# First head mixing as three float32r passes, with a hi/lo split of the gathered scores

## Chip, cores, metric
One core of a Trainium2 chip. The metric is the device time of one launch in microseconds (us), the median of several runs; lower is better.

## What is computed
Two batches, 12 heads, 448 positions, head size 64. Scores are mixed over the heads, go through a softmax, are mixed over the heads again and multiply v; two feed-forward blocks follow. The part before them:

```python
scores = scale * np.matmul(q, k.transpose(0, 1, 3, 2))
scores = np.einsum('bhij,hg->bgij', scores, w_pre)
scores = scores - np.max(scores, axis=-1, keepdims=True)
attn = np.exp(scores)
attn = attn / (np.sum(attn, axis=-1, keepdims=True) + 1e-09)
attn = np.einsum('bhij,hg->bgij', attn, w_post)
return np.matmul(attn, v).astype(np.float32)
```

## The kernel before
Queries of a batch are cut into four tiles of 120, 120, 120 and 88 rows (`tiles`, index `ti`). `qk` (L134) makes the raw scores of two heads of a tile with float32 matmuls. `qk_out` (L145) copies them to SBUF, the even head on ScalarE (L153), the odd one on VectorE (L151), into one of four `s` buffers, and SyncE's DMA queue scatters them into a gather tile `G` (two of them, used by even and odd tiles) whose partitions hold 10 query rows times 12 heads. The 88-row tile needs three DMAs per head (L157, L165) where the others need one.

The mixing then runs over 46 pairs of such groups (`PAIRS`, `plist`): 6, 6, 6 and 5 pairs per batch; a tile's pair index r is 0 for its first pair, and the 88-row tile's last pair holds one group only. `premix` (L167) multiplies a group by the head weights in one float32 matmul, which the trace shows as two records. `smin` (L176, VectorE) and `sexp` (L183, ScalarE) are the softmax, `weights2` (L193, VectorE) folds 1/sum into the second mixing weights w2, `post` (L208) is the second mixing, and `evac` (L225) copies its result out, half on ScalarE and half on VectorE. `av` (L245) multiplies by v, `av_out` (L259) copies that out.

Slot n of the main loop (L429) does: premix of pair n+1, `qk_out`, post of pair n, softmax of pair n+1, evac of n, weights2 of n+1, and then what hand-written tables put there (`at`, L302): `qk` of the next tile, `av` of the tile before, loads. `load_v` (L128) for the second batch is in the table of slot 29; it follows that slot's scatters on the DMA queue, and the first user is `av` in slot 30. In slots 37 to 43 (`dve_l`, and L413) ScalarE, VectorE and GpSimd also split the first weights of the feed-forward part and the attention output of batch 0 into float32r hi and lo parts (L372, L377, L401, L402). Every engine works strictly in the order of this program.

The feed-forward part (`stage`, L468; `mm`, L445) already multiplies in three float32r passes, hi·hi, hi·lo and lo·hi.

Of the kernel before, what the change touches and what calls it, by code (L numbers as in the profile page):

```python
# [8 lines left out]
F32R = mybir.dt.float32r  # L9
# [3 lines left out]
ALU = mybir.AluOpType  # L13
AX = mybir.AxisListType

B, H, S, D = 2, 12, 448, 64
# [11 lines left out]
GP = 128  # L28
JP = 112
NJ = S // JP  # L30
NC = DM // 128
# [8 lines left out]
PAIRS = []  # L40
# [12 lines left out]
def place(k, h):  # L53
    return 64 if (k, h) == (ROW - 1, H - 1) else PK * k + h
# [3 lines left out]
def attention_moe_kernel(  # L58
# [10 lines left out]
    nc = tc.nc  # L69
    ctx.enter_context(tc.manual_schedule())  # L70

    const = ctx.enter_context(tc.tile_pool(name="const", bufs=1))
# [4 lines left out]
    def ps(tag):  # L77
        return psum.tile([128, 512], F32, tag=tag, name=tag, bufs=PB[tag])

    def rd(ap):  # L80
        return ap.bitcast(F32)


    wpre_sb = const.tile([128, 128], F32, name="wpre_sb")
    wp = const.tile([128, H, KG], F32, name="wp")

    def single(tag, dtype=F32R):
        return outer.tile([128, S], dtype, tag=tag, name=tag)
# [10 lines left out]
    att = ExitStack()  # L99
    sb = att.enter_context(tc.tile_pool(name="att", bufs=1))  # L100
    s_p = att.enter_context(tc.tile_pool(name="s", bufs=4))
    e_p = att.enter_context(tc.tile_pool(name="e", bufs=2))
    a_p = att.enter_context(tc.tile_pool(name="a", bufs=2))

    G = [sb.tile([128, H, S], F32, name=f"G{i}") for i in range(2)]
    A = {}
    E = {}
    Z = {}
    W2 = {}
# [22 lines left out]


    def qk(b, t, c, tags=("qk", "qk")):  # L134
        n = ROWS[t]
        p = [ps(tag) for tag in tags]
        for e in range(2):
            o = 64 * e
            nc.tensor.matmul(  # L139
                p[e][0:n, 0:S], qq[b, t][o:o + 64, c * TILE:c * TILE + n], kk[b, c][o:o + 64, :], start=True, stop=True  # L140
            )
        for e in range(2):
            Sps.append((b, t, 2 * c + e, p[e]))

    def qk_out(stage=None):  # L145
        while Sps:
            b, t, h, p = Sps.pop(0)
            n = ROWS[t]
            s = stage[h // 2][0:TILE, h % 2, :] if stage else s_p.tile([TILE, S], F32, tag="s", name="s")
            if h % 2:  # L150
                nc.vector.tensor_copy(s[0:n], p[0:n, 0:S])  # L151
            else:
                nc.scalar.copy(s[0:n], p[0:n, 0:S])  # L153
            g = G[t % 2]
            full = n // ROW
            last = ROW - 1 if h == H - 1 else ROW
            nc.sync.dma_start(out=g[h:PK * (last - 1) + h + 1:PK, 0:full, :], in_=s[0:last * full])  # L157
            if last < ROW:
                o = place(last, h)
                nc.sync.dma_start(out=g[o:o + 1, 0:full, :], in_=s[last * full:ROW * full])  # L160
            rem = (n - full * ROW) // 2
            for f in range(2 if rem else 0):
                o = full * ROW + f * rem
                a = place(f * KG, h)
                nc.sync.dma_start(out=g[a:a + PK * (rem - 1) + 1:PK, full, :], in_=s[o:o + rem])  # L165

    def premix(b, m):  # L167
        t, r, n = PAIRS[m]
        for i in range(n):
            p = ps("T")  # L170
            nc.tensor.matmul(  # L171
                p[0:GP, 0:S], wpre_sb[0:GP, 0:GP], G[t % 2][0:GP, r + i, :], start=True, stop=True
            )
            Tps[b, m, i] = p

    def smin(b, m, i):  # L176
        if i == 0:
            NB[b, m] = e_p.tile([128, 2], F32, tag="nb", name="nb")
        nc.vector.tensor_reduce(  # L179
            out=NB[b, m][0:GP, i:i + 1], in_=Tps[b, m, i][0:GP, 0:S], op=ALU.min, axis=AX.X  # L180
        )

    def sexp(b, m, i):  # L183
        if i == 0:
            Z[b, m] = e_p.tile([128, 2], F32, tag="z", name="z")
        e = e_p.tile([128, S], F32, tag=f"e{i}", name="e")
        nc.scalar.activation(  # L187
            out=e[0:GP], in_=Tps.pop((b, m, i))[0:GP, 0:S], func=ACTF.Exp, bias=NB[b, m][0:GP, i:i + 1], scale=-1.0,
            accum_out=Z[b, m][0:GP, i:i + 1],
        )  # L190
        E[b, m, i] = e

    def weights2(b, m):  # L193
        n = PAIRS[m][2]
        z = Z.pop((b, m))[0:GP, 0:n]
        NB.pop((b, m))
        w2 = e_p.tile([128, 2, H * KG], F32, tag="w2", name="w2")
        nc.vector.tensor_scalar(z, z, 1e-9, None, ALU.add)
        nc.vector.reciprocal(out=z, in_=z)
        nc.vector.tensor_tensor(  # L200
            out=w2[0:GP, 0:n, :],
            in0=wp[0:GP].rearrange("p (o g) k -> p o (g k)", o=1).to_broadcast([GP, n, H * KG]),
            in1=z.rearrange("p (n o) -> p n o", o=1).to_broadcast([GP, n, H * KG]), op=ALU.mult,
        )
        W2[b, m] = w2


    def post(b, m):  # L208
        t, r, n = PAIRS[m]
        w2 = W2.pop((b, m))  # L210
        p = [ps("post") for _ in range(2)]
        k = H * KG
        for i in range(n):
            e = E.pop((b, m, i))
            for j in range(NJ):
                for f in range(2):
                    o = 64 * f
                    c = (i * NJ + j) * k
                    nc.tensor.matmul(  # L219
                        p[f][0:JP, c:c + k], e[o:o + 64, j * JP:(j + 1) * JP], w2[o:o + 64, i, :],  # L220
                        start=True, stop=True,
                    )
        Pps[b, m] = p

    def evac(b, m, f):  # L225
        t, r, n = PAIRS[m]
        if r == 0 and f == 0:
            A[b, t] = a_p.tile([JP, NJ * H, TILE], F32, tag="a", name="a")
        a = A[b, t]
        p = Pps[b, m][f]  # L230
        k = half_rows(t, r + n - 1)
        src = p[0:JP, 0:n * NJ * H * KG].rearrange("p (n g k) -> p n g k", n=n, k=KG)[:, :, :, 0:k]
        o = r * ROW + f * k
        dst = a[:, :, o:o + (n - 1) * ROW + k]
        if n == 2:
            dst = a[:, :, r * ROW:(r + 2) * ROW].rearrange("p g (n i) -> p n g i", n=2)[:, :, :, f * KG:f * KG + KG]
        else:
            src = src[:, 0]
        if f:
            nc.vector.tensor_copy(dst, src)  # L240
        else:
            nc.scalar.copy(dst, src)


    def av(b, t, c):  # L245
# [5 lines left out]
        for j in range(NJ):  # L251
            for e in range(2):
                g = 2 * c + e
                nc.tensor.matmul(  # L254
                    p[64 * e:64 * e + 64, o:o + n], vv[b][:, j, g * D:(g + 1) * D], A[b, t][:, j * H + g, 0:n],
                    start=(j == 0), stop=(j == NJ - 1), skip_group_check=True,
# [17 lines left out]
    nc.gpsimd.memset(G[0], 0.0)  # L274
    nc.vector.memset(G[1], 0.0)
    nc.vector.tensor_scalar(wpre_sb, wpre_sb, -0.125, None, ALU.mult)


    def busy(n):
# [16 lines left out]
    plist = [(b, m) for b in range(B) for m in range(NPB)]  # L296
    span = [sum(1 for x in PAIRS if x[0] == t) for _, t in tiles]
    base = [sum(span[:i]) for i in range(len(tiles))]
    NS = len(plist)
    act_l, dve_l, mid = {}, {}, {}  # L300

    def at(d, slot, *f):  # L302
        d.setdefault(max(slot, 0), []).append(f)

    for ti, (b, t) in enumerate(tiles):
        s0, sp = base[ti], span[ti]
        if ti + 1 < len(tiles):
            nxt = tiles[ti + 1]
            for c in range(NC):
                at(mid, s0 - 3 + c if ti else (c * (sp - 3)) // NC, qk, *nxt, c)  # L310
            if ti + 2 < len(tiles):
                at(mid, s0 - 2, load_q, *tiles[ti + 2])
            if nxt[1] == NTL - 1 and nxt[0] + 1 < B:
                for c in range(NC):
                    at(mid, s0 + c // 2, load_k, nxt[0] + 1, c)
        if ti > 0:
            pb, pt = tiles[ti - 1]
            for c in range(NC):
                s = s0 + 1 + (c * (sp - 1)) // NC
                at(mid, s, av, pb, pt, c)  # L320
                if c % 2:
                    at(mid, s, av_out, pb, pt, c // 2)
            if pt == NTL - 1 and pb + 1 < B:
                at(mid, s0 + sp, load_v, pb + 1)
# [80 lines left out]
    s0 = base[-1]  # L405
# [10 lines left out]
    def run(d, n):  # L416
        for f in d.get(n, []):
            f[0](*f[1:])

    def softmax(n):  # L420
        b, m = plist[n]
        for i in range(PAIRS[m][2]):
            smin(b, m, i)
            sexp(b, m, i)

    premix(*plist[0])
    softmax(0)
    weights2(*plist[0])
    for n in range(NS):  # L429
        if n + 1 < NS:  # L430
            premix(*plist[n + 1])
        qk_out()
        post(*plist[n])
        if n + 1 < NS:
            softmax(n + 1)
        run(act_l, n)
        evac(*plist[n], 0)
        evac(*plist[n], 1)
        if n + 1 < NS:
            weights2(*plist[n + 1])  # L440
        run(dve_l, n)
        run(mid, n)
# [204 lines left out]
```

## Time and profile before

| | us |
|---|---|
| median of 3 runs (771.75 to 772.64) | 772.56 |
| the profiled execution | 769.89 |
| its span, first to last instruction | 768.1 |
| attention part, to the first feed-forward matmul | 262.82 |
| TensorE busy in the span | 745.7 (97%) |
| TensorE's share of the chain that ended last | 95% |
| VectorE / ScalarE / GpSimd busy | 487.4 / 309.1 / 18.0 |

The sum of the prediction is made against the profiled execution, which is shorter than the median of the runs; the span lies inside it with 1.79 us around it. "PE" is TensorE's matmuls, "PEld" its weight loads, "DVE" VectorE, "ACT" ScalarE, "POOL" GpSimd, "SPq" the DMA issues of SyncE.

### The profile page before, as it was taken

Reading aid. Unit: us, or ns where it says so; the run is one execution under the profiler, and the core shown is the slowest. Engines: PE = TensorE matmul, PEld = TensorE weight load, DVE = VectorE, ACT = ScalarE, POOL = GpSimd, SP = SyncE. Lnnn points to the kernel's source line nnn. Section 1 sums busy time; section 2 is a strip of 40 time slices with the busy share of each in tenths; the row PEclk is TensorE's granted clock in tenths of the full one; section 3 lists DMA queues with packets and bytes.
Section 4 is the critical chain, followed back from the end, with each engine's and each line's share of the span. In section 5 each row is a group of like instructions: output and inputs, shape, how many; then the busy total and the mean of one; then the engine's idle time right before and its main releaser. Section 6 shows DMA issues by size and latency. Waiting matters only on the chain.

```text
span 768.1 us, 12411 instructions
## 1 busy us (share of the span) xinstructions
PE 745.7 (97%) x5055; PEld 617.8 (80%) x5055; DVE 487.4 (63%) x817; ACT 309.1 (40%) x559; POOL 18.0 (2%) x16
## 2 busy tenths in 40 slices
PE   6799999998999999999999999999999999999998
PEld 2356666665667799999999999999999999999997
DVE  4366656565667767676667666556888888654540
ACT  2355554454456443334333323223555554322220
POOL 3000000000002300000000000000000000000000
PEclk9799999999999999999999999999999999999999
DMA  6543243426141113323323323323233332434310
GB/s 215 170 132 102 82 129 116 120 74 188 57 146 58 61 65 125 123 83 123 124 83 124 123 83 124 124 82 124 83 123 101 106 124 88 160 129 134 126 48 36
DMA packets 26696, 84.85 MB, mean 110 GB/s; under 512 B 2896, under 2 KB 16736, under 8 KB 26416
## 3 DMA queue, kind: packets, MB, share of 16 engines
q1 hardware_dynamic: 26496, 83.59, 33.2%
q8 instruction: 40, 0.66, 0.4%
q0 software_dynamic: 144, 0.47, 0.2%
q14 instruction: 16, 0.13, 0.0%
HBM read 62.03 MB, written 2.75 MB: 84 GB/s over the span
## 4 chain that ended last, share of the span: by engine, by line
PE 95%; DMA 2%; SPq 1%; DVE 1%; ACT 0%; issue 0%; ACTq 0%; POOLq 0%
PE T L171 10%; PE post L219 10%; PE T L448 8%; PE T L449 8%; PE T L450 8%; PE qk L448 5%; PE post L449 5%; PE post L448 5%; PE post L450 5%; PE qk L449 5%; PE qk L450 5%; PE av L254 5%; PE qk L139 5%; PE av L450 3%; PE av L449 3%; PE av L448 3%
## 5 line engine op out<-in xcount | busy, mean ns | idle before, releaser
L372 ACT CAST wh<-wc 128x768 fp32r<-128x768 f32 x68 | 56.8, 835 | 122.3 <-DVE wc L366 108.8
L219 PEld LDWEIGHTS post<-w,e 64*112 64x112 f32 x1440 | 74.4, 174 | 29.8 <-PE T L171 21.5
L377 DVE TENSOR_TENSOR wl<-wc,wh 128x768 fp32r<-128x768 f32 x66 | 63.0, 955 | 48.1 <-ACT wh L372 48.1
L187 ACT ACTIVATE e<-T,nb 128x448 f32<-128x448 f32 x90 | 56.9, 633 | 88.0 <-DVE nb L179 87.9
L171 PE MATMUL T<-G,wpre_sb 128*128 128x448 f32 x180 | 82.3, 581 | 8.4 <-DMA G<-x 8.4
L449 PE MATMUL T<-m,wh 128*128 128x448 f32 x237 | 86.6, 365 | 0.0
L448 PE MATMUL T<-m,wh 128*128 128x448 f32 x237 | 86.6, 365 | 0.0
L450 PE MATMUL T<-m,wl 128*128 128x448 f32 x237 | 86.5, 365 | 0.0
L219 PE MATMUL post<-w,e 64*112 64x60 f32 x1440 | 80.5, 261 | 0.1
L179 DVE TENSOR_REDUCE nb<-T 128x1 f32<-128x448 f32 x90 | 55.8, 623 | 28.3 <-PE T L171 23.4
L171 PEld LDWEIGHTS T<-G,wpre_sb 128*128 128x128 f32 x180 | 31.6, 195 | 47.4 <-issue 46.1
L355 DVE SCALAR_TENSOR_TENSOR wa<-wr,wa 128x768 uint32<-128x768 uint32 x68 | 65.2, 959 | 2.3
L366 DVE SCALAR_TENSOR_TENSOR wc<-wc,wa 128x768 uint32<-128x768 uint32 x68 | 65.2, 958 | 2.3
L240 DVE COPY a<-post 112x480 f32<-112x480 f32 (+1 forms) x46 | 30.9, 671 | 49.6 <-PE post L219 49.6
L350 ACT ACTIVATE wc<-wr 128x768 f32<-128x768 f32 x68 | 61.4, 903 | 0.0
L254 PE MATMUL av<-a,v 112*64 112x120 f32 (+1 forms) x768 | 45.2, 264 | 5.2 <-DMA v<-v 3.0
L254 PEld LDWEIGHTS av<-a,v 112*64 112x64 f32 x768 | 37.0, 136 | 15.7 <-PE post L219 4.0
L362 DVE TENSOR_SCALAR wc<-wc 128x768 f32<-128x768 f32 x68 | 38.7, 569 | 16.3 <-ACT wc L350 16.3
L139 PE MATMUL qk<-ks,q 64*120 64x448 f32 (+1 forms) x176 | 44.9, 568 | 4.1 <-DMA q<-qT 2.3
L448 PEld LDWEIGHTS T<-m,wh 128*128 128x128 f32 x237 | 44.5, 188 | 3.5
L449 PEld LDWEIGHTS T<-m,wh 128*128 128x128 f32 x237 | 44.5, 188 | 3.5
L450 PEld LDWEIGHTS T<-m,wl 128*128 128x128 f32 x237 | 44.5, 188 | 3.5
(146 smaller groups left out, 1353.2 us busy)
## 6 DMA issues: line engine op xcount, KB each, us to landing
wr<-w SPq DMA_DIRECT2D x68, 768.0 KB
G<-s SPq DMA_DIRECT2D x55, 210.0 KB
G<-s SPq DMA_DIRECT2D x22, 140.0 KB
ks<-kT SPq DMA_DIRECT2D x12, 224.0 KB
v<-v SPq DMA_DIRECT2D x2, 1344.0 KB
outT<-ta SPq DMA_DIRECT2D x12, 224.0 KB
q<-qT SPq DMA_DIRECT2D x7, 360.0 KB
G<-x SPq DMA_DIRECT2D x11, 210.0 KB
```

The source lines that it names most:

```text
L139: nc.tensor.matmul(p[e][0:n, 0:S], qq[b, t][o:o + 64, c * TILE:c * TILE + n], kk[b, c][o:o + 64, :], start=True, stop=True)
L171: nc.tensor.matmul(p[0:GP, 0:S], wpre_sb[0:GP, 0:GP], G[t % 2][0:GP, r + i, :], start=True, stop=True)
L187: nc.scalar.activation(out=e[0:GP], in_=Tps.pop((b, m, i))[0:GP, 0:S], func=ACTF.Exp, bias=NB[b, m][0:GP, i:i + 1], scale=-1.0, accum_out= ...
L219: nc.tensor.matmul(p[f][0:JP, c:c + k], e[o:o + 64, j * JP:(j + 1) * JP], w2[o:o + 64, i, :], start=True, stop=True,)
L254: nc.tensor.matmul(p[64 * e:64 * e + 64, o:o + n], vv[b][:, j, g * D:(g + 1) * D], A[b, t][:, j * H + g, 0:n], start=(j == 0), stop=(j == ...
L350: nc.scalar.activation(out=st["c"], in_=rd(st["high"]), func=ACTF.Abs, scale=HSC)
L355: nc.vector.scalar_tensor_tensor(out=a, in0=st["high"], scalar=0x80000000, in1=a, op0=ALU.bitwise_and, op1=ALU.bitwise_or)
L366: nc.vector.scalar_tensor_tensor(out=cu, in0=cu, scalar=3, in1=st["a"], op0=ALU.logical_shift_left, op1=ALU.bitwise_or)
L377: eng.tensor_tensor(out=lo, in0=st["c"], in1=rd(st["hi"]), op=ALU.subtract)
L448: nc.tensor.matmul(p[:, 0:S], hi[:, sl], x[0], start=first, stop=False)
L449: nc.tensor.matmul(p[:, 0:S], hi[:, sl], x[1], start=False, stop=False)
L450: nc.tensor.matmul(p[:, 0:S], lo[:, sl], x[0], start=False, stop=last)
```

## The change
The head weights are split once into `wpre_hi` and `wpre_lo`. Each gathered group is split by `split_g`: ScalarE casts it to float32r (hi), GpSimd subtracts (lo). `premix` becomes hi·hi, lo·hi and hi·lo in one PSUM accumulation. The split of pair n+2 is issued in slot n, ahead of `qk_out`'s copies, or behind them where the pair is its tile's first. `qk` of the next tile moves one slot earlier, and calls `qk_out` first, so that a slot with several `qk` copies the earlier ones at once. There is one hi buffer per group index and two lo buffers.

```diff
+    wpre_hi = const.tile([128, 128], F32R, name="wpre_hi")
+    wpre_lo = const.tile([128, 128], F32R, name="wpre_lo")
...
+    g_p = att.enter_context(tc.tile_pool(name="g", bufs=2))
...
     def qk(b, t, c, tags=("qk", "qk")):
+        qk_out()
...
+    def split_g(b, m):
+        t, r, n = PAIRS[m]
+        for i in range(n):
+            src = G[t % 2][:, r + i, :]
+            hi = g_p.tile([128, S], F32R, tag=f"gh{i}", name="gh", bufs=1)
+            lo = g_p.tile([128, S], F32R, tag=f"gl{i}", name="gl")
+            nc.scalar.copy(hi, src)
+            nc.gpsimd.tensor_tensor(out=lo, in0=src, in1=rd(hi), op=ALU.subtract)
+            GG[b, m, i] = (hi, lo)
...
-            nc.tensor.matmul(
-                p[0:GP, 0:S], wpre_sb[0:GP, 0:GP], G[t % 2][0:GP, r + i, :], start=True, stop=True
-            )
+            hi, lo = GG.pop((b, m, i))
+            nc.tensor.matmul(p[:, 0:S], wpre_hi, hi, start=True, stop=False)
+            nc.tensor.matmul(p[:, 0:S], wpre_lo, hi, start=False, stop=False)
+            nc.tensor.matmul(p[:, 0:S], wpre_hi, lo, start=False, stop=True)
...
+    nc.scalar.copy(wpre_hi, wpre_sb)
+    nc.vector.tensor_tensor(out=wpre_lo, in0=wpre_sb, in1=rd(wpre_hi), op=ALU.subtract)
...
-                at(mid, s0 - 3 + c if ti else (c * (sp - 3)) // NC, qk, *nxt, c)
+                at(mid, s0 - 4 + c if ti else c // 2, qk, *nxt, c)
...
+    split_g(*plist[0])
     premix(*plist[0])
+    split_g(*plist[1])
     softmax(0)
...
+        k = n + 2 < NS and PAIRS[plist[n + 2][1]]
+        if k and k[1]:
+            split_g(*plist[n + 2])
         qk_out()
+        if k and k[1] == 0:
+            split_g(*plist[n + 2])
         post(*plist[n])
```

The order of instructions moves. ScalarE's in two slots around the start of the second 88-row tile's scores, before (L153 the score copy, L187 the exponentials, L242 the evacuation):

```order
L153 COPY s<-qk 120x448
L187 ACTIVATE e,z<-T,nb 128x448 x2
L242 COPY a<-post 112x2x48x5
L153 COPY s<-qk 88x448
L187 ACTIVATE e,z<-T,nb 128x448 x2
L242 COPY a<-post 112x2x48x5
```

and in the change (L179 is the new cast, L158 the score copy, L204 the exponentials, L259 the evacuation), in the slot of a pair inside a tile and in that of a tile's first pair:

```order
L179 CAST gh<-G_89 128x448 x2
L158 COPY s<-qk 88x448
L204 ACTIVATE e,z<-T,nb 128x448 x2
L259 COPY a<-post 112x2x48x5
L158 COPY s<-qk 88x448
L179 CAST gh<-G_88 128x448 x2
L204 ACTIVATE e,z<-T,nb 128x448 x2
```

Two casts now stand ahead of the exponentials in every slot, and ahead of the score copy in all but a tile's first.

SyncE's DMA queue around the load of v for the second batch, before:

```order
L157 DMA G_83<-s 10x12x448 x2
L121 DMA q<-qT 128x720
L157 DMA G_83<-s 10x12x448 x4
L130 DMA v<-v 112x3072
L157 DMA G_83<-s 10x12x448 x5
```

and in the change:

```order
L162 DMA G_88<-s 10x12x448 x4
L125 DMA q<-qT 128x720
L162 DMA G_88<-s 10x12x448 x4
L134 DMA v<-v 112x3072
L162 DMA G_88<-s 10x12x448 x3
```

The load of v still follows the scatter of the slot it stands in; eight heads are ahead of it now, six before, since the scores come one slot earlier.

GpSimd in the last slots of attention, in the change (before, only the rows of L377 and L402, here L396 and L421, were there; `gl` is the new lo part):

```order
L180 TENSOR_TENSOR gl<-G_89,gh 128x448 x4
L396 TENSOR_TENSOR wl<-wc,wh 128x768
L421 TENSOR_TENSOR ks_3042<-x_0_759,ks_3041 128x448
L421 TENSOR_TENSOR ks_3046<-x_0_759,ks_3045 128x448
L180 TENSOR_TENSOR gl<-G_89,gh 128x448 x2
L421 TENSOR_TENSOR ks_3103<-x_1_895,ks_3102 128x448
L180 TENSOR_TENSOR gl<-G_89,gh 128x448 x2
```

The lo parts of the last pairs stand behind the splits of weights and attention output.

## Rows read from the trace of the kernel before

**Rows 1.** Chain in order of time, two kinds of slot: start us, us, what.

```profile
54.28 0.81 PE qk L139 x4
...
111.32 1.70 PE T L171 x4
113.02 1.72 PE post L219 x32
114.74 0.97 PE av L254 x16
115.71 0.95 PE qk L139 x4
```

**Rows 2.** The same chain, first float32r passes of the feed-forward part.

```profile
262.82 0.40 PE qk L448
263.22 0.20 PE qk L449
```

**Rows 3.** Timeline of a slot: start us, us, engine line op out<-in [idle before <-releaser].

```profile
113.03 0.63 ACT L187 ACTIVATE e<-T,nb 128x448 f32<-128x448 f32 x1 [1.14 <-DVE nb L179]
...
114.77 0.64 ACT L242 COPY a<-post 112x480 f32<-112x480 f32 x1 [0.32 <-PE post L219]
...
115.39 0.15 DVE L198 TENSOR_SCALAR z<-z 128x2 f32<-128x2 f32 x1
...
115.78 0.28 DVE L200 TENSOR_TENSOR w<-wp,z 128x120 f32<-128x120 f32 x1
...
116.68 0.53 ACT L153 COPY s<-qk 120x448 f32<-120x448 f32 x1 [1.27 <-PE qk L139]
...
117.64 1.38 DVE L179 TENSOR_REDUCE nb<-T 128x1 f32<-128x448 f32 x2 [0.29 <-PE T L171]
```

**Rows 4.** Timeline near the end of attention, splits on ScalarE and GpSimd.

```profile
242.03 0.83 ACT L372 CAST wh<-wc 128x768 fp32r<-128x768 f32 x1
...
242.76 1.03 ACT L401 CAST ks<-x 128x448 fp32r<-128x448 f32 x2
...
242.94 1.81 POOL L377 TENSOR_TENSOR wl<-wc,wh 128x768 fp32r<-128x768 f32 x1 [235.35 <-ACT wh L372]
...
244.72 2.23 POOL L402 TENSOR_TENSOR ks<-x,ks 128x448 fp32r<-128x448 f32 x2
...
246.50 0.47 DVE L198 TENSOR_SCALAR z<-z 128x2 f32<-128x2 f32 x1
...
251.00 2.98 POOL L402 TENSOR_TENSOR ks<-x,ks 128x448 fp32r<-128x448 f32 x2 [2.00 <-ACT ks L401]
```

**Rows 5.** Chain at the start of attention.

```profile
19.20 3.83 DMA G<-x
...
23.44 5.89 PE T L171 x8
...
32.47 1.50 PE qk L139 x4
```

**Rows 6.** Load of v for the second batch: timeline, chain, and TensorE's waits.

```profile
179.44 1.77 PE L171 MATMUL T<-G,wpre_sb 128*128 128x448 f32 x4
181.86 9.06 DMA v<-v
PE av L254 <- DMA v<-v: 3.0, 1, 3.0
```

**Rows 7.** TensorE's timeline, then busy time by stretch; PEclk is the granted clock.

```profile
11.43 3.60 PE L282 MATMUL av<-warm 128*1 128x448 f16 x18
18.50:18.75 0.25, 0.00 (x0) 0.00 (x0) 0.00 (x0) 0.00 (x0) 0.00 (x0) 0.57 0.62 186
28.75:29.00 0.25, 0.25 (x2) 0.00 (x0) 0.25 (x2) 0.00 (x0) 0.00 (x0) 0.95 0.03 12
```

**Rows 8.** SyncE's queue, first and last issues of the first 88-row tile's scatter.

```profile
80.62 0.77 SPq L157 DMA_DIRECT2D G<-s  x1
...
111.04 1.24 SPq L165 DMA_DIRECT2D G<-s  x2
```

More of the change, by code (lines that the diff above doesn't have):

```diff
@@ L103, in attention_moe_kernel @@
     a_p = att.enter_context(tc.tile_pool(name="a", bufs=2))
+    g_p = att.enter_context(tc.tile_pool(name="g", bufs=2))
     G = [sb.tile([128, H, S], F32, name=f"G{i}") for i in range(2)]
     A = {}
+    GG = {}
     E = {}
```

## Prediction

> **What bounds the kernel now.** I read the page first: TensorE holds 95% of the chain that ended last, so what TensorE does between two waits is the time. The feed-forward part is not touched; the change lies in the attention part, before 262.82 us. Second, the chain in order of time [rows 1]: a slot is premix 1.70, post 1.72, av 0.97, qk 0.95, which follow each other without a hole: 5.34 us. A slot without av (a tile's first, and slots 3 to 6) is 1.70 + 1.72 + 0.81 = 4.23. Third, the timeline of the other engines in a slot [rows 3], to see how much room they have behind TensorE. Last, the four places where the chain leaves TensorE or will: the start [rows 5], the load of v [rows 6], the 88-row tiles' scatter [rows 8], and the slots that also split weights [rows 4].
>
> **Premix.** Two groups cost 1.70 [rows 1], four records. The same form as the new passes stands at the start of the feed-forward part: 0.40 for the first pass, whose weights are not yet loaded, then 0.20 each [rows 2]. Six passes: 0.40 + 5 x 0.20 = 1.40. Saving 0.30 per pair, 0.15 for the two single groups. Of 44 double pairs, four lie in the start (below): 40 x 0.30 + 2 x 0.15 = **12.3 us**, if nothing else ends later. Lower end: a first-pass price of 0.40 for each of the two groups makes 1.60, so 0.10 per pair, 4.2 us.
>
> **Does a regular slot still fit?** Put t = 0 at the start of premix, whose passes then end at 0.4, 0.6, ... 1.4. ScalarE's casts of pair n+2 need the single hi buffers, which the second pass of each group frees at 0.6 and 1.2. Two casts took 1.03 [rows 4], so they run 0.7 to 1.8; then the score copy, 0.53 [rows 3], to 2.35; two exponentials, 0.63 each with some 0.1 for the accumulator, to 3.8; evacuation 0.64, to 4.45. GpSimd: two subtracts took 2.23 [rows 4], so 1.35 to 3.6; they are wanted at t = 1.2 of the next slot. VectorE: minima 1.38 from 0.85 on, evacuation behind post (3.1) to 3.9, weights2 from z's 0.15 to w2's 0.28 [rows 3], 0.67 in all: to 4.6. The next post starts at 5.04 + 1.40, or at 3.92 + 1.40 = 5.3 without av. So casts, subtracts and everything behind the casts on ScalarE cost **0**; their cover is 0.7 us in slots without av and 1.8 with it. ScalarE is then busy 3.7 of 3.9 us in the short slots.
>
> **Start.** The two wpre splits stand ahead of the first score copies and push the first scatter back about 0.25 (a 128-column cast, estimated at half the 0.52 one). Then hi, lo and three passes in a row replace one matmul. But TensorE runs at half clock there: eight records take 5.89 [rows 5]. Twelve passes at 0.4 are 4.8, and the casts and subtracts of four groups, 0.55 and 1.1 each, interleave with them: the last lo of pair 1 is ready at about 28.6, its last pass at 29.2, and w2 of pair 0 at 29.3. Before, the first post started at 29.33. Cost 0.1. In slots 0 to 2, TensorE already waits for ScalarE's copy between two qk (1.50 where 0.85 is normal [rows 5]). The exponentials now end 0.6 after post instead of before it, so this copy is 0.4 to 0.5 later, which eats the 0.30 (that is why four pairs are left out), and the first qk of tile 2 moves into slot 2: 0.95 more and another wait of 0.5. A later slot has one qk less (0.8). Net **-0.7** (ends 0 to -2).
>
> **Load of v.** In slot 29 the load is queued behind that slot's scatter. Before, the slot starts at 179.44 and the load goes out at 181.86, at t = 2.42; it takes 9.06, and av in slot 30 waits 3.0 for it [rows 6]. Now the score copy stands behind two casts and ends at 2.35 instead of 0.63; two scatter issues of 0.8 (0.77 in [rows 8]) follow, so v goes out at t = 4.05 and lands at 13.1. TensorE gets to that av after two short slots, 2 x 3.92 = 7.85. The wait is 5.25: **-2.2 us** (ends 0, if the load runs faster, to -3).
>
> **The clock there.** The profile shows what such a hole does: TensorE stopped at 15.03 (11.43 + 3.60), and between 18.50 and 18.75 the granted clock went to half, 1.2 GHz. It took up work at 23.44 [rows 5] and had the full 2.4 GHz back at about 28.75 [rows 7], after 5.3 us of work. A hole of 5.25 is longer than those 3.5, so I take it that the clock falls, and 5.3 us of work then do half of it: **-2.65** (other end 0).
>
> **Last slots.** From slot 40 on, GpSimd's lo parts stand behind the split of weights (1.81) and of attention output (2.23 for two). With t = 0 at slot 39: lo of pair 42 until 7.7; the weight cast follows ScalarE's evacuation (8.0 + 0.83 [rows 4]), its subtract ends at 10.75, two output parts at 13.05, and only then the two lo of pair 43, 14.2 and 15.35. TensorE has premix 43 in slot 42, at 4.1 + 4.1 + 3.1 = 11.3, and wants the second lo at 12.5. It waits 2.9 in all; by slot 43 the queues have caught up. **-2.9** (ends -1 to -5, with subtracts of 1.49 as in the slower two of [rows 4]).
>
> **Sum.** 12.3 - 0.7 - 2.2 - 2.65 - 2.9 = 3.85 us gained. Against the profiled execution, 769.89, that gives 766.0. It ran 2.67 below the median of the runs, 772.56, and I carry the difference over: **768.7**.
>
> **A rule that speaks against it.** When GpSimd's two subtracts ran from 244.72 to 246.95, weights2's z operation, normally 0.15 [rows 3], took 0.47 and ended with them [rows 4]. The Trainium skill (SBUF — State Buffer, SBUF: two separate sides) says that GpSimd shares one pair of ports with some VectorE operations, as an exclusive lock held for the whole instruction. The trace agrees with that in this row.
>
> **Rivals.**
> 1. *The clock does not fall at the v load*, or recovers at once. For it: one hole of 3.0 and one of 8 us say little about 5.25, and if the load lands 1 us earlier the hole is hardly longer than 3.5. Then 768.7 - 2.65 = 766.0.
> 2. *The holes stay shut*: the load of v lands as early as before and GpSimd catches up. Only the 0.7 is lost: 772.56 - 11.6 = 761.0. Against it: the orders of the two queues are fixed.
> 3. *z behind a subtract in every slot.* If GpSimd ends 0.5 later than worked out, weights2 starts behind the second subtract, up to 1.1 later, which is 0.4 more than the cover of a short slot; ten of those: 4.4. 768.7 + 4.4 = 773.1. Against it: by the times above GpSimd ends at 3.6 and z starts at 3.9.
> 4. *Slower: the scatter of the 88-row tiles.* The first one kept SyncE's queue from 80.62 to 112.28 [rows 8], 31.7 us for 36 issues and the loads between. Its first issue must now wait until GpSimd has read that G's last old group (t = 3.6 of its slot, 0.6 before), seven slots are 2.0 shorter, and the reader is a cast almost a slot earlier. With a landing of 3.83 as in [rows 5] the cast is 0 to 1.1 us late, against a cover of 1.8. Beyond 1.8 TensorE waits, and behind the cast on ScalarE the exponentials too. At 5.5 late for both such tiles it is 2 x 3.7 = 7.4: 776.1. It decides for slower than before from about 3.8 late.
> 5. *The three passes cost as much as float32.* The rows of the feed-forward part [rows 2] exclude that.
>
> **How the numbers follow.** Forecast 0.38, rival 1 0.22, rival 2 0.12, rival 3 0.10, rival 4 0.18. A measurement of this kernel tells about 0.2%, 1.5 us, from no change: faster is below 771.0, slower above 774.1. Forecast, rival 1 and rival 2 are faster unless the premix saving is at its lower end, which I give 0.06 of them; rival 3 is mostly the same, rival 4 slower but for a few hundredths. Faster 0.67, same 0.13, slower 0.20. The range leaves out most of rival 2 and the far end of rival 4: 763.0 to 775.5. The forecast's own range is 766 to 772.
>
> **What would show it.** Passes of premix 0.40 and 0.20 in the chain; a regular slot of 5.04; av of batch 1 waiting 5 us for v, with half clock behind it; premix waiting for GpSimd near the end, some 3 us; no wait of post for w2 in regular slots; the feed-forward part as long as before. It is wrong if regular slots hold waits for ScalarE or GpSimd, if casts wait for G's scatter for more than 2 us, or if TensorE's clock is down anywhere else.

## The result, and the profile after

The change is slower: 776.92 us in the median of 20 runs (773.41 to 787.6) against 771.76 for the kernel before (769.37 to 781.08); the ratio is 1.0077, 95% interval 1.0054 to 1.0100. The forecast of 768.7 and the range up to 775.5 were wrong. Medians and ranges here hold all runs; the ratios leave out those more than 1.5% above the fastest run of their kernel.

In some executions, of kernels with and without the change, the feed-forward passes take 0.2064 us each in place of 0.2025 at the same granted clock, which adds 9.8 us; the profiled execution of the change is one, and half of the change's runs, at 773.4 to 775.2, are inside the range but still above the median before.

The stretches of that pace stand in the profile by themselves. Busy time from 300 to 700 us, the change (PE busy with its passes in brackets, then PEld, DVE, ACT and POOL, the granted clock, the DMA share, GB/s):

```profile
300.00:700.00 400.00, 400.00 (x1938) 363.32 (x1937) 277.34 (x390) 154.42 (x229) 0.00 (x0) 1.00 0.31 107
```

and the kernel before:

```profile
300.00:700.00 400.00, 400.00 (x1975) 370.77 (x1974) 282.16 (x395) 156.19 (x231) 0.00 (x0) 1.00 0.34 113
```

400/1938 is 0.2064, 400/1975 is 0.2025. So I compare attention alone, at the start of the last pair's post (pair 45; this start and those of the other slots are read from TensorE's timeline): 260.86 us before, **265.98** in the change, 5.12 later. From there to the end it is 507.2 and 517.0, and the 9.8 between them is the pace. The profiled execution took 784.77, 14.88 above the 769.89 of before, which is 5.12 + 9.8 to within 0.1.

**A regular slot** is what was predicted. The chain of waits in order of time (start, us, what), the change, against [rows 1]:

```profile
83.21 1.71 PE post L236 x32
84.93 0.97 PE av L271 x16
85.90 0.92 PE qk L144 x4
86.82 0.40 PE T L188
87.22 0.21 PE T L189
...
88.25 1.72 PE post L236 x32
```

From post to post it is 5.04 where 5.31 stood before. The passes cost 0.40 + five of 0.20 or 0.21, 1.43 for a pair, as in [rows 2], and no hole stands between them. Where, then, was it lost? The table follows the two profiles by the start of each slot's post, the change minus before:

| from slot to slot | change over it, us | what lies there |
|---|---|---|
| start of slot 0 | -0.08 | the casts and subtracts at the start |
| 0 to 4 | +3.07 | scores of the third tile, `s` buffers, clock |
| 4 to 19, 21 to 30, 31 to 37, 38 to 41 | -8.43 | 33 regular slots |
| 19 to 21 | +0.64 | two qk in slot 19, one less in 20 |
| 30 to 31 | +4.62 | load of v, clock |
| 37 to 38 | -1.06 | one qk less |
| 41 to 45 | +6.36 | premix behind GpSimd, clock |
| sum | +5.12 | |

**Slots 0 to 4.** VectorE's waits in the change from 36 to 60 us (engine, line, what it waited for: total, times, longest):

```profile
DVE s L156 <- DMA G<-s: 5.8, 3, 2.1
```

and what the chain makes of it:

```profile
43.14 3.74 DMA G<-s
...
46.97 0.64 DVE s L156
...
47.65 1.01 PE qk L144 x2
```

Slot 2 now holds three qk, whose copies need six `s` buffers where there are four; VectorE's copies wait until a scatter has read theirs, and the third qk until the copy has emptied its bank. The kernel before has no such wait of VectorE between 36 and 60. TensorE's own waits in the same stretch of the change are short:

```profile
PE qk L144 <- ACT s L158: 1.4, 3, 0.6
PE qk L144 <- DVE s L156: 0.4, 1, 0.4
```

Before, it waits 1.2 us there, in two.

**The load of v.** It goes out at 181.62, 4.1 after the start of the premix of its slot, as predicted. The two scatters in front of it on the queue start when ScalarE's score copy has ended (179.37 + 0.53); from the timeline:

```profile
179.92 1.61 SPq L162 DMA_DIRECT2D G<-s  x2
```

and the chain behind it:

```profile
181.62 9.73 DMA v<-v
191.35 0.04 issue
191.40 3.47 PE av L271 x32
```

TensorE waited 5.9 us, where [rows 6] had 3.0. An av of 32 matmuls takes 1.79 to 1.86 at full clock.

**The last slots.** The chain leads through GpSimd, in the order that was predicted:

```profile
242.00 1.84 POOL wl L396
243.84 2.20 POOL ks L421 x2
246.04 1.10 POOL gl L180
247.14 0.04 issue
247.18 0.74 PE T L190
...
249.07 3.18 PE post L236 x32
252.25 3.40 PE av L271 x32
```

The pass that multiplies the lo part waited 2.0 us for GpSimd. What follows is twice as long as in a regular slot: post 3.18 for 1.71, av 3.40 for 1.79. The clock says why. Busy time by stretch, the change (columns as above; the value behind the POOL column is the granted clock, where 1.00 is 2.4 GHz and 0.50 is 1.2 GHz):

```profile
49.00:53.00 4.00, 4.00 (x36) 3.32 (x34) 1.80 (x3) 2.81 (x7) 2.25 (x2) 0.58 0.26 83
...
189.00:195.00 6.00, 3.60 (x33) 3.30 (x34) 0.08 (x1) 0.00 (x0) 0.00 (x0) 0.50 0.24 78
195.00:198.00 3.00, 3.00 (x34) 2.58 (x36) 2.10 (x4) 2.00 (x5) 1.40 (x2) 0.88 0.00 0
...
247.00:257.00 10.00, 9.82 (x72) 8.57 (x73) 7.37 (x11) 4.20 (x10) 7.81 (x7) 0.50 0.11 15
```

The kernel before holds the full clock in all three places:

```profile
36.00:58.00 22.00, 20.77 (x192) 12.16 (x190) 13.32 (x31) 12.39 (x29) 0.00 (x0) 1.00 0.44 138
180.00:196.00 16.00, 12.98 (x148) 8.55 (x146) 7.72 (x18) 6.66 (x17) 0.00 (x0) 1.00 0.56 163
240.00:258.00 18.00, 17.92 (x235) 13.42 (x234) 13.66 (x30) 12.48 (x29) 9.64 (x7) 1.00 0.14 46
```

Work lost to the clock, busy time multiplied by what is missing of 1.00: 4.00 x 0.42 = 1.7 in slots 2 and 3; 3.60 x 0.50 + 3.00 x 0.12 = 2.2 at the load; 9.82 x 0.50 = 4.9 at the end. Together 8.8 us, as much as the passes save in the 33 regular slots (8.43). It is an estimate from these rows. The prediction had 2.65 for it, in one place.

### The profile page after: what moved, and what is told of

The parts are those of the page before. It is cut to its first block, busy times and chain, and to the rows that moved or that the text cites. A ratio compares the mean times of both kernels' runs of the same rounds, so it can differ in the third digit from the quotient of the medians.

```text
span 783.0 us, 12825 instructions
## 1 busy us (share of the span) xinstructions
PE 755.7 (97%) x5145; PEld 642.4 (82%) x5145; DVE 489.9 (63%) x818; ACT 346.2 (44%) x650; POOL 118.6 (15%) x106
## 4 chain that ended last, share of the span: by engine, by line
PE 91%; DMA 3%; DVE 2%; ACT 2%; POOL 1%; SPq 1%; issue 0%; ACTq 0%; DVEq 0%; POOLq 0%
PE post L236 9%; PE T L474 8%; PE T L476 8%; PE T L475 8%; PE qk L474 5%; PE post L476 5%; PE qk L476 5%; PE post L475 5%; PE post L474 5%; PE qk L475 5%; PE av L271 5%; PE qk L144 5%; PE T L188 3%; PE av L476 3%; PE av L475 3%; PE av L474 3%
## 5 line engine op out<-in xcount | busy, mean ns | idle before, releaser
L180 POOL TENSOR_TENSOR gl<-G,gh 128x448 fp32r<-128x448 f32 x90 | 100.7, 1138 | 139.3 <-ACT gh L179 139.2
L396 DVE TENSOR_TENSOR wl<-wc,wh 128x768 fp32r<-128x768 f32 x66 | 63.0, 955 | 49.6 <-ACT wh L391 49.6
L236 PEld LDWEIGHTS post<-w,e 64*112 64x112 f32 x1440 | 76.5, 179 | 14.7 <-PE T L189 12.7
L179 ACT CAST gh<-G 128x448 fp32r<-128x448 f32 x90 | 50.6, 566 | 81.0 <-PE T L189 65.1
L236 PE MATMUL post<-w,e 64*112 64x60 f32 x1440 | 82.7, 265 | 0.2 <-DVE w L217 0.2
L204 ACT ACTIVATE e<-T,nb 128x448 f32<-128x448 f32 x90 | 56.2, 631 | 4.1 <-DVE nb L196 4.0
L271 PE MATMUL av<-a,v 112*64 112x120 f32 (+1 forms) x768 | 48.4, 276 | 8.5 <-DMA v<-v 5.9
L271 PEld LDWEIGHTS av<-a,v 112*64 112x64 f32 x768 | 39.9, 144 | 15.5 <-DMA v<-v 6.7
L144 PE MATMUL qk<-ks,q 64*120 64x448 f32 (+1 forms) x176 | 47.2, 574 | 5.2 <-DMA q<-qT 2.6
```

The lines of the kernel that those rows point to most:

```text
L144: nc.tensor.matmul(p[e][0:n, 0:S], qq[b, t][o:o + 64, c * TILE:c * TILE + n], kk[b, c][o:o + 64, :], start=True, stop=True)
L180: nc.gpsimd.tensor_tensor(out=lo, in0=src, in1=rd(hi), op=ALU.subtract)
L236: nc.tensor.matmul(p[f][0:JP, c:c + k], e[o:o + 64, j * JP:(j + 1) * JP], w2[o:o + 64, i, :], start=True, stop=True,)
L271: nc.tensor.matmul(p[64 * e:64 * e + 64, o:o + n], vv[b][:, j, g * D:(g + 1) * D], A[b, t][:, j * H + g, 0:n], start=(j == 0), stop=(j == ...
L396: eng.tensor_tensor(out=lo, in0=st["c"], in1=rd(st["hi"]), op=ALU.subtract)
```

## The experiments

The theory after this reading: the passes and the casts do what they were meant to; the change loses at three places, where it puts off something that TensorE needs (the third qk in slot 2, the load of v, the lo part behind GpSimd's splits), and each hole costs as much again in clock. The rival: the casts and subtracts themselves, or the earlier scores, cost the time all over, and moving other things will not bring it back. The edits are made to the change, except where another kernel is named; the expectations were written before the runs.

### The load of v one slot earlier

```diff
-                at(mid, s0 + sp, load_v, pb + 1)
+                at(mid, s0 + sp - 1, load_v, pb + 1)
```

> Only the load of v for the second batch moves, from slot 29 to the end of slot 28, ahead of slot 29's scatter. Theory (three holes, each with a fall of the clock behind it): the load goes out about 4 us earlier in its slot, av waits 1.5 to 2 us for it instead of 5.9, the granted clock stays at 2.4 GHz there, and 4.0 + 2.0 = 6 us are gained over the change: some 768 where the change has 774, slightly faster than before. Rival (the loss is spread over the slots by the casts and subtracts, and the hole only shows it): under 1 us gained.

Measured 767.75 us (765.54 to 770.94, 10 runs), ratio to before 0.9966, interval 0.9948 to 0.9985. The last pair's post starts at 257.64, 8.34 earlier than in the change; from slot 30 to slot 31 alone it takes 6.02 where the change took 13.72, 7.7 less. The chain at the load:

```profile
176.44 8.82 DMA v<-v
185.26 0.04 issue
185.31 1.86 PE av L271 x32
```

The wait is 0.2 us, av 1.86 and not 3.47. This alone turns the loss into a small gain. At the end of attention the wait of 2.0 for GpSimd stays, and the clock falls behind it for 10 us again. From 47 to 56 us, though, it stays at 1.00 in this profile, with the same instructions and the same waits of TensorE in slots 2 and 3 as in the change.

### The scores of the third tile one slot later

```diff
-                at(mid, s0 - 4 + c if ti else c // 2, qk, *nxt, c)
+                at(mid, s0 - (4 if ti != 1 else 3) + c if ti else c // 2, qk, *nxt, c)
```

> Only the scores of the third tile (index 2) go back to the slots they had before, 3 to 8 instead of 2 to 7, so slot 2 holds two qk and not three. Theory: VectorE's score copies no longer wait for an s buffer (5.8 us in three waits), TensorE has no gaps before slot 3, the clock does not fall at 49, and 1.5 + 1.9 = 3.4 us are gained over the change: about 770.5 where the change has 774. Rival (the clock falls there for another reason, the waits are covered): under 1 us.

Measured 774.11 us (772.62 to 781.09, 10 runs), ratio 1.0062, interval 1.0033 to 1.0090: the expected gain of 3.4 did not come. Slot 3 starts 2.67 earlier than in the change, and then the slots from 4 on lose more: at slot 19 it is 5.43 behind the change. Premix waited for GpSimd's lo part there; TensorE's waits from 48 to 75 us:

```profile
PE T L190 <- POOL gl L180: 0.7, 2, 0.5
PE post L236 <- DVE w L217: 0.2, 1, 0.2
```

Behind these small holes the clock was down for nearly 14 us:

```profile
58.00:73.00 15.00, 15.00 (x107) 10.96 (x104) 7.15 (x16) 8.09 (x20) 6.08 (x6) 0.54 0.19 59
```

ScalarE stands idle for 2.7 us ahead of the first cast of the next tile, whose last scatter is now issued late:

```profile
51.71 1.64 SPq L162 DMA_DIRECT2D G<-s  x2
54.02 1.03 ACT L179 CAST gh<-G 128x448 fp32r<-128x448 f32 x2 [2.68 <-PE post L236]
```

The profile puts the end of that wait down to post, which the cast does not need; that it is the scatter is likely, but not shown. The hole had moved, not closed. The fall of the clock does not belong to the edit: the kernel with all three edits (below) has the same waits at the same place, 0.7 in two and 0.2, and its clock stays at 1.00 there.

### The attention output's splits two slots later

```diff
-        at(mid, s0 - 1 + (2 * i) // 3, split_x0, i)
+        at(mid, s0 + 1 + (i + 1) // 2, split_x0, i)
```

> Only the split of batch 0's attention output moves later, from slots 40 to 43 to slots 42 to 45, behind the lo parts of the last pairs on GpSimd. Theory: premix of pair 43 no longer waits 2.0 us for GpSimd, the clock does not fall at 247 for 10 us of work, and 2.5 + 4.9 = 7 us are gained over the change: about 767. Rival (the output's split then holds up the start of the feed-forward part by as much as it spared): within 1 us of the change.

Measured 769.35 us (767.9 to 776.48, 10 runs), ratio 0.9992, interval 0.9970 to 1.0014. Some 767 was expected. GpSimd's queue is free when the last lo parts are due. The clock stays up at the end:

```profile
240.00:247.00 7.00, 7.00 (x89) 5.86 (x88) 6.59 (x16) 4.79 (x10) 3.42 (x4) 1.00 0.33 119
247.00:257.00 10.00, 9.59 (x134) 8.08 (x134) 7.36 (x18) 8.98 (x21) 8.24 (x7) 1.00 0.01 2
```

From slot 41 to 45 it takes 16.73 us, in the change 23.15: 6.4 recovered there, 2.0 the wait and the rest the clock and what hung on it. Its profiled execution lost much of that again in slots 3 to 6, where the clock was down from 50 to 68 us and not to 53 only, though the order of the instructions up to there is that of the change. The early fall thus differs between executions of the same early instructions: 17 us here, 3.4 in the change, none with the load of v moved.

### All three, and two of them

> The three moves together. Theory: 6 + 3.4 + 7 = 16 us over the change, about 757.5 where the change has 774 and before 771.8, a ratio of 0.982; what is left is the premix saving of 0.27 per pair over nearly all 44 pairs plus 1 to 2 us of the shorter v wait. Rival (holes move to the next place): 765 or more.

> The load of v and the split of batch 0's output moved, the scores left where the change has them. After the third move alone gave nothing, the theory is that it only carried the gap from slot 2 to slot 4, where the first cast of tile 1 waits for the scatter; then this is as fast as all three, 760 to 763. If the move of the scores does help once the other holes are gone: 764 or more.

All three edits: 761.08 us (759.26 to 767.08, 5 runs), ratio 0.9890, interval 0.9851 to 0.9928; 757.5 was expected. Without the later scores, so with the load and the splits alone: 761.61 us (760.38 to 774.79, 5 runs, three of them below 762), ratio 0.9861, interval 0.9837 to 0.9886. The two are alike; the last pair's post starts at 251.90 and 252.41. Two edits of the tables put the changed kernel some 10 us below the kernel before by these medians, 8.45 by the profiles of attention.

### The same two edits without the change

The kernel before has the load of v where the change has it, and a wait of 3.0 for it. Does the gain belong to the change at all? First the load alone, in the kernel before; then both moves.

> The kernel before with only its load of v moved to the end of slot 28. Its 3.0 us wait should shrink to 0.5: 2.4 us gained, 768.5. If the load is bound by the scatter's traffic and not by when it goes out: no gain.

> The kernel before with both moves. The old kernel has no hole at the output split, so this should be as its load of v alone gave, 767; then the change itself, with the same moves, is worth 767 less 761.6 = 5.5 us, and not the 10 us that lie between its moved version and the kernel before.

The load alone gives 767.13 us (766.3 to 768.48, 4 runs), ratio 0.9945, interval 0.9926 to 0.9965. The last pair's post starts 3.7 us earlier (257.13); 3.1 of that comes at the load, as the wait is gone, and 0.6 is there at slot 0 already, ahead of the edit. Both give 768.16 us (766.65 to 778.4, 10 runs), ratio 0.9992, interval 0.9958 to 1.0027; the profiled execution has the longer feed-forward pace, 1937 passes in 400 us, so attention alone says more. Its last pair's post starts at 256.86. So with equal tables the change brings 256.86 - 252.41 = 4.45 us in attention. Slot 0 starts at 28.22 here and at 30.01 in the change with both moves; from slot 0 on the change brings 6.24. The rest of its lead is the load of v.

### What the passes are worth alone

On the kernel with two edits, premix becomes the old matmul again:

```diff
-            nc.tensor.matmul(p[:, 0:S], wpre_hi, hi, start=True, stop=False)
-            nc.tensor.matmul(p[:, 0:S], wpre_lo, hi, start=False, stop=False)
-            nc.tensor.matmul(p[:, 0:S], wpre_hi, lo, start=False, stop=True)
+            nc.tensor.matmul(p[:, 0:S], wpre_sb, G[t % 2][:, r + i, :], start=True, stop=True)
```

> As the one before, but the first mixing is the old float32 matmul from G; casts and subtracts still run and nothing reads them. Theory (the passes give what the rows say, 0.27 per pair, and casts and subtracts cost nothing where there is no hole): 40 pairs x 0.27 = 11 us slower than with the passes, 772 to 774, about as before or 2 us above it. Rival (much of the gain of the moved kernel comes from the moves alone): under 6 us slower, below 769.

Measured 789.8 us (781.92 to 792.97, 4 runs), ratio 1.0222, interval 1.0174 to 1.0271. It says nothing of the passes, because it brought a wait of its own:

```profile
PE T L188 <- DMA G<-s: 7.7, 4, 2.6
```

With the scores a slot earlier the next scatter into the same `G` stands ahead of the premix of a tile's last pair. A premix that reads `G` itself has to wait for that scatter, and then finds the first scores of a later tile in it. The control with the same waits as the change reads the hi part, and leaves the lo part out, in place of the three passes:

```diff
+            nc.tensor.matmul(p[:, 0:S], wpre_sb, rd(hi), start=True, stop=True)
```

> The change with both loads moved (v one slot earlier, the attention output's splits two slots later), its casts and subtracts as they are, but premix again one float32 matmul per group, of the whole weights with the hi part; the pass over the lo part is left out of what is computed. This is the control that the earlier one failed to be, since premix now waits for the same cast as in the change. Theory: the passes save 0.27 us per pair wherever TensorE is the bound, in some 42 pairs, so this kernel takes 761.6 + 11 = 772.6, a regular slot is 5.30 long again, and the earlier places of the scores and the casts cost the rest of the difference to the kernel before with both moves, 772.6 - 767.5 = 5, all of it in the first slots. Rival: the holes of the first slots swallow what the passes save there and behind the load, so that the passes are worth no more than the 6 us between the two kernels with both moves: 767.5.

Measured 778.51 us (773.94 to 789.43, 11 runs), ratio 1.0067, interval 1.0044 to 1.0091, against 0.9861 for the same kernel with passes; 772.6 was expected. Its chain in a short slot, against passes of 0.40 + five of 0.20 or 0.21:

```profile
102.42 1.72 PE post L234 x32
104.14 0.78 PE qk L144 x4
104.92 1.70 PE T L188 x4
106.62 1.72 PE post L234 x32
```

4.20 here; 3.95 with passes. From slot 6 to slot 41 it takes 181.09 us, with passes 171.49: 9.60 over 35 slots, 0.274 each. That is the expected price, and the rival (6 us in all) falls. Casts and subtracts cost next to nothing over these slots: the kernel before with both moves, which has the same float32 matmuls and neither these nor the earlier scores, takes 180.33 from slot 6 to slot 41, 0.76 less than the control. That settles the other rival, a cost all over. The excess over 772.6 lies, as far as the one profile tells, in slots 2 to 5, where the clock was down from 49 to 63 us, and in its longer feed-forward pace.

### Work in the hole ahead of av

```diff
+            if pt == 0 and pb == 1:
+                at(mid, s0 + 1, busy, 14)
```

> The change with 14 idle matmuls (0.2 us each, results unused) ahead of the av that waits for v; the load itself is not touched. Theory: the hole of 5.9 us is as long as before, but TensorE stands still for about 3 of it only, the granted clock stays at 2.4 GHz there, and the 2.0 us that the half clock cost are gained: about 772 where the change has 774. Rival (the fall costs nothing, the hole all): same as the change.

Fourteen matmuls whose result nobody uses stand ahead of the waiting av, so that only part of the hole is left. Measured 777.29 us (773.82 to 779.49, 6 runs), ratio 1.0069, interval 1.0042 to 1.0096; 772 was expected, and it is no faster than the change. TensorE's wait, and the clock by stretch:

```profile
PE av L271 <- DMA v<-v: 3.3, 1, 3.3
```

```profile
188.00:191.00 3.00, 0.08 (x1) 0.00 (x0) 0.00 (x0) 0.00 (x0) 0.00 (x0) 1.00 0.53 180
191.00:195.00 4.00, 3.61 (x33) 3.34 (x34) 0.16 (x1) 0.00 (x0) 0.00 (x0) 0.57 0.03 9
```

The clock still fell, later and for 3.4 us rather than 6.8. From slot 30 to slot 31 that gave 0.2 us; a load sent one slot earlier gave 7.7.

### More score buffers

```diff
-    s_p = att.enter_context(tc.tile_pool(name="s", bufs=4))
+    s_p = att.enter_context(tc.tile_pool(name="s", bufs=6))
...
-    g_p = att.enter_context(tc.tile_pool(name="g", bufs=2))
+    g_p = att.enter_context(tc.tile_pool(name="g", bufs=1))
```

on the kernel with two edits, and on that with all three. The single lo buffers make room.

> The two moves (load of v, output split) with six s buffers instead of four; the lo parts have one buffer instead of two to make room. Theory of the start: VectorE's score copies in slots 2 and 3 wait 5.4 to 5.8 us in three waits for an s buffer, so they go; the step from slot 2 to slot 3 against the kernel before falls from 2 to 4 us to the 1.3 us of the third qk, and the clock falls there less often: 759 to 760, a ratio near 0.984. Rival (SyncE's queue of scatters is the limit, and the wait turns up at the first cast of tile 1): as without it, 761.6, 0.986.

> The same with the third tile's scores in their old slots as well, so slot 2 has two qk. If the s buffers were the limit: the step at slot 3 is gone and the one at slot 5 too, 758 to 759. If SyncE's queue is: still a step of 1.2 at slot 5, 760 to 761.

Two edits: 768.49 us (759.32 to 770.36, 12 runs), ratio 0.9929, interval 0.9893 to 0.9965. The expected 759 to 760 is that of its profiled execution, 760.68, whose last pair's post starts at 251.50. All three: 769.8 us (758.95 to 775.69, 12 runs), ratio 0.9930, interval 0.9891 to 0.9969, last pair's post at 250.80; its profile has the longer feed-forward pace, 1937 passes in 400 us. With two edits VectorE's copies wait for no scatter any more; from 49 to 53 the clock holds:

```profile
49.00:53.00 4.00, 4.00 (x44) 2.96 (x42) 1.87 (x3) 2.25 (x6) 1.66 (x2) 1.00 0.57 189
```

From slot 0 to slot 6 it takes 31.77 us, in the kernel with two edits 34.19, and 31.68 before. The first slots are mended. With all three edits the loss of 1.2 at slot 5 against the kernel before stays, with six buffers as with four, and with it TensorE's waits of 0.7 for the lo part: that was the sign noted for SyncE's queue as the limit there. But the start of slot 0 came at 31.44 with two edits and six buffers, 1.43 later than with four, so only 0.9 of the 2.4 arrives at the last pair. By the medians the buffers gained nothing; that they are worth 1 us rests on the profiles alone.

## Why the prediction was wrong

**Premix, right in kind, 1.7 us too large.** 12.3 us were expected, 0.30 a pair. The 33 regular slots gave 8.43, some 0.27 a slot where nothing else differs; with 0.27 for eight more inside the disturbed places (2.2) it is 10.6. The pass is 0.20 to 0.21, so a pair is 1.43 and not 1.40. The control says 0.274.

**Does a regular slot still fit, right.** ScalarE's casts cost 0.57 and GpSimd's subtracts 1.14 each in the mean, and TensorE waits for neither in a regular slot. Rival 3 stayed out of the regular slots. Its mechanism appears in slot 41, where GpSimd splits weights and attention output; VectorE's timeline in the change:

```profile
245.27 0.80 DVE L215 TENSOR_SCALAR z<-z 128x2 f32<-128x2 f32 x1
...
246.30 0.97 DVE L217 TENSOR_TENSOR w<-wp,z 128x120 f32<-128x120 f32 x1
```

z took 0.15 and w 0.28 in [rows 3]. They ended at 246.07 and 247.27, just behind a GpSimd instruction each (246.04 and 247.14 in the chain above). The rule of the Trainium skill (SBUF — State Buffer, SBUF: two separate sides), an exclusive lock on shared ports for a whole instruction, agrees with these rows too.

**Start, undersized.** Predicted loss 0.7, which included one qk less in slot 37. Measured: -0.08 for the first post; 3.07 in slots 0 to 4; 0.64 + 2 x 0.27 = 1.2 in slots 19 to 21; -1.06 + 0.27 = -0.8 in slot 37. Together 3.4, of which 1.7 is clock. Without the clock it is 1.7. What I overlooked is the number of `s` buffers: I counted TensorE's wait for ScalarE's copy, not VectorE's for the scatter. Nor did I see what happens in slot 19: the 88-row tile has five slots for the next tile's six qk, so one slot holds two, slot 20 before and slot 19 now, where the second takes 2.12 and not 1.22. The -0.08 of the first post is a favourable pair of profiles: slot 0 starts at 29.18 to 31.44 in the nine profiles that have the passes, the change's own being the earliest, and at 28.22 to 29.26 in the three without splits. So the start likely costs some 1 us more than this table shows, where 0.1 was predicted; why, and why it varies so, is open.

**Load of v, right.** The wait rose by 2.9 us (predicted 2.2; the load took 9.73, not 9.06), the clock cost 2.2 (predicted 2.65). With the premix saving set aside, slot 30 to 31 lost 4.62 + 0.27 = 4.9; 2.2 + 2.65 is 4.85. Rivals 1 and 2 fall here: the clock fell, and the hole opened.

**Last slots, right in the wait, wrong in the clock.** Premix waited 2.0 (predicted 2.9), at the pass and behind the queue that were named. But slots 41 to 45 lost 6.36 + 4 x 0.27 = 7.4, of which 4.9 is clock.

**The step that failed is "The clock there".** It charged the clock at one place, the load of v, on the ground that its hole is longer than the 3.5 us from TensorE's stop to the fall in [rows 7], and let shorter holes pass. The runs showed it lowered for 10 us behind the wait of 2.0, in all four profiles that have this wait, and not in the profiles where the splits were moved and the wait is gone; it was lowered behind a wait of 3.3; and in slots 2 and 3 behind waits of 0.2 to 0.6 each, in three of the five profiles that have the change's instructions there (the change, the moved splits, the two edits; not with the load alone moved or the hole filled). Behind the 3.0 of [rows 6] it was not. The prediction had itself listed a lowered clock anywhere else as a sign that it is wrong. The sum was 3.85 us gained and came out 5.12 lost, 9.0 apart. The clock makes 8.8 - 2.65 = 6.2 of that, the premix saving 1.7, the start without clock 1.0; what remains of the load of v (0.5 more) and of the last slots (0.4 less) nearly cancels. Rival 4, the only one well on the slower side, was not what happened: behind the first cast the profile of the change shows no cast that waits for a scatter. So the direction failed as well: I had given slower 0.20, nearly all of it to a mechanism that stayed away, and none to a second or third fall of the clock.

Beside this, the pace of the feed-forward passes makes the ratio look worse than attention is; it lay outside the prediction.

## What to carry to other kernels

A hole in TensorE's work can cost more than its length, by the work that runs at half clock behind it: here 4.9 us behind a wait of 2.0. So when an operation is made cheaper, first look for each transfer and each side queue that was just in time before, and send those earlier, or move what stands ahead of them; here one line of a table was worth 7.7 us and the faster passes 4 to 6. And compare the stage that was edited beside the medians: another stage can differ by more than the edit does.

## What was not expected of the hardware, and what stays open

Which holes lower the clock. Their length does not put the cases in order: 3.0 us idle left the clock at 1.00, 2.0 us lowered it for 10 us, and the same early instructions, with the same waits of TensorE to within 0.2 us, lowered it for 3.4 us in two profiles, for 17 us in a third and not at all in two more. So a single profile does not tell whether an edit brought such a fall or avoided it. Whether the subtract's 2.0-us wait would spare the clock with other work around it was not tried.

The feed-forward passes have two paces, 0.2025 and 0.2064 us, at a granted clock of 1.00 and with the same instructions. In the change's profile the first block of 18 passes, ahead of the last av, goes at the shorter and everything behind it at the longer. What selects it is not known. It was seen in kernels with the change (its own profile) and without it (that with both moves), so the change is not its cause; how often it comes seems to go with the program as built (7 of 20 runs of the change lie at 783 us or more, 4 of 10 of the kernel before with both moves at 775.7 or more, but only one of the 100 runs of the kernel before above 775), though not every one of these runs was profiled.
